# Upper table rows from GpSimd's DMA queue, four matmuls for the last half of T, more idle matmuls, a moved w_out step and two transform steps per PSUM bank

## The chip, the cores and the metric

The kernel runs on one core of a Trainium2 chip. The metric is the device time of one execution in microseconds (us), as a median over runs. PE is TensorE, DVE is VectorE, ACT is ScalarE, POOL is GpSimd, SP is the engine that issues most DMAs.

## What is computed

The reference chains three operators over 24576 rows of 256 numbers (8 sequences of 3072):

```python
X = np.fft.fft(np.fft.fft(x, axis=1), axis=2).real      # x: 8 x 3072 x 256, float32
logits = X @ phi                                        # 32 slots, 8 experts x 4
d = exp(logits - logits.max(0)); d /= d.sum(0) + 1e-9   # softmax over all tokens
slot_out[e] = maximum((d.T @ X)[e] @ w1[e], 0) @ w2[e]
c = exp(logits - logits.max(1)); c /= c.sum(1) + 1e-9   # softmax over slots
y = c @ slot_out
out = (s * maximum(y @ w_in, 0)**2 + b) @ w_out         # w_in 256 x 2048, w_out 2048 x 256, float64
```

## The kernel before, in words

The transform is not computed for 256 columns. `x` is projected with the DFT-transformed `phi` to 32 slot columns, the sequence transform is done on these, and the logits come out of it. The stages follow one another on PE:

- **V** (about 12 to 84 us). `emit_v` (L382) multiplies pages of `x` (`xb`, 1 MB each, 24 of them, three to a batch) with the projected `phi`; part 0 of a batch needs pages x0 and x2, part 1 page x1. `turn_v` (L408) transposes the result. `pump_a` (L316) issues loads in the order of the string `ORDER` (L297): x is a page of `x`, w a quarter of `w_out` (float64, turned into float32 on DVE by `double_steps`), r a page of `x` for a later stage (`xrt`), l a part of the table `ltab`, h a part of `htab`. All of these are issued on SP's queue, at most eight outstanding.
- **T.** `emit_t` (L423) does the 128-point transform of a batch and writes `tt`. For the last batch it is split: four matmuls (L428) and eight copies on ACT (L432) for the first half of the steps, 32 matmuls of a 32x32 tile each (L439) and two DVE copies (L445) for the last half. `keep_warm` (L187) issues matmuls on a tile of ones that nobody reads; `WARM` = 4 of them follow T (L519).
- **L** (90 to 106 us). 16 half steps (L570) multiply `ltab` with `tt`, the two halves of the rows (0 to 63 and 64 to 127) beside each other. Both need the same table, so the rows 64 to 127 of `ltab` are a copy of rows 0 to 63, made by POOL (L512, L513). For each half step ACT copies the PSUM bank to `lg` (L583) and DVE takes the maximum (L585).
- **The maximum** (L592 to L610). The maximum over all tokens is put together: a transpose to `mt` (L598), a reduction to `cm2` (L603), a diagonal `dg` (L605), a matmul `mb` (L607) that spreads it over the partitions, a copy to `cmb` (L608). 8, 3 and 8 idle matmuls lie between (L596, L599, L610). Ahead of `cm2`, the loop at L600 empties `side_work`: at that point it holds the two steps `low` of the last quarter of `w_out` (L216 on DVE), which also give back a page.
- **H** (114.5 to 142 us). 16 steps: `emit_d` subtracts the maximum (L633, DVE and POOL in turn), ACT takes the exponential (L669), four matmuls with a part of `htab` (L652) fill two PSUM tiles of 208 columns, and `h_out` (L639) copies one on ACT and one on DVE to `hh` (L643).
- **R** (142 to 204 us). Transposes, a transform and sums with the 24 pages `xrt` (L704 to L731); each page that is used up is loaded anew, and after the `xrt` come `w_in`, `w1` and `w2`. **E** (to 236 us) are the experts. **F** is the last operator, 64 blocks of 384 tokens, until the end at 1411.6 us.

The pages of 8 KB per partition come from a ring of 15, later 20, and a load waits until the page's last user is done. Engines run their instructions in the order in which the program issued them.

Of the kernel before, what the change touches and what calls it, by code (L numbers as in the profile page):

```python
# [32 lines left out]
def tile_fft2__then__softmoe__then__act_relu2(  # L33
# [261 lines left out]
    WARM = 4  # L295
# [50 lines left out]
    def htab_load(i):  # L346

        t, k = page([R, 16, 2, 4 * MH], F32, "htab_t")
        htabs.append((t, k))
        nc.gpsimd.memset(t[32:64], 0.0)  # L350
        for q in range(2):
            nc.sync.dma_start(out=t[64 * q:64 * q + M], in_=htab[:, 32 * i:32 * i + 32].rearrange("r (k q) m -> r k q m", q=2))
        dma_ready(2.5)
# [5 lines left out]
    def ltab_load(i):  # L359
        t, k = page([P, 32, P // 2], F32, "ltab")  # L360
        ltabs.append((t, k))
        for c in range(2):
            nc.sync.dma_start(out=t[NR * c:NR * c + NR], in_=ltab[64 * c:64 * c + M, 32 * i:32 * i + 32].rearrange(
                "(j g) q m -> g j q m", j=2)[0:NR // 2])
        dma_ready(2.57)

    with tc.tile_pool(name="xtp", bufs=1, side="right") as xtp, tc.tile_pool(name="vp", bufs=1, side="right") as vp, \
# [55 lines left out]
        def emit_t(b):  # L423
            bg, bq = divmod(b, NG)
            if b == B - 1:
# [8 lines left out]
                t = psv.tile([P, 2, 4, 64], F32, tag="vt", name="tpb", bufs=2)  # L434
                for k in range(4, 8):
                    for j in range(4):
                        for c in range(2):
                            q = 64 * (j // 2) + NR * c
                            nc.tensor.matmul(t[q:q + NR, j % 2, k - 4, :], lhsT=vs[bg][:, bq, 4 * k + j, :],  # L439
                                             rhs=f_sb[:, 64 * c:64 * c + 64], start=True, stop=True,  # L440
                                             tile_position=(0, q), skip_group_check=True)
                for eh in range(2):
                    src = t[64 * eh:64 * eh + 64].rearrange("p j k m -> p m j k")
                    dst = tt[64 * bg:64 * bg + 64, :, bq, 16 * eh:16 * eh + 16].rearrange("p m (j k) -> p m j k", j=2)
                    nc.vector.tensor_copy(dst[:, :, :, 4:8], src)  # L445
# [66 lines left out]
        nc.gpsimd.tensor_copy(ltabs[0][0][64:P], ltabs[0][0][0:64])  # L512
        nc.gpsimd.tensor_copy(ltabs[1][0][64:P], ltabs[1][0][0:64])  # L513
# [44 lines left out]
    with tc.tile_pool(name="ps_l", bufs=6, space=PSUM) as psl, \  # L558
# [37 lines left out]
        keep_warm(warm, 8)  # L596
        mt = psm.tile([NE, R], F32, tag="mt", name="mt")
        nc.tensor.transpose(mt, cm1, ident[:R, :R])  # L598
        keep_warm(warm, 3)  # L599
        while side_step(0.0, True):  # L600
            pass
# [8 lines left out]
        keep_warm(warm, 8)  # L610
# [13 lines left out]
    with tc.tile_pool(name="ps_h", bufs=3, space=PSUM) as psh:  # L624
# [14 lines left out]
        def h_out(i):  # L639
            for q in range(2):  # L640
                hpv = hps[i][q].rearrange("p k (q c m) -> p (k q) c m", q=2, c=2)
                eng = nc.vector.tensor_copy if q else nc.scalar.copy
# [667 lines left out]
```

## Time and profile before

| | us |
|---|---|
| median of three runs (1397.17 to 1401.28) | 1400.21 |
| span of the profiled execution | 1411.6 |
| of it V, T and their start (to the first L570) | 90.3 |
| L and the maximum (to the first L652) | 24.3 |
| H | 27.6 |
| R and E (to 236 us) | 94 |
| F | 1175 |

The profiled execution is one execution, and its span, from its first instruction to its last, is 11.4 us longer than the median of the runs. PE is busy in 98% of the span, but busy says nothing of the clock: the row PEclk of the page is the share of TensorE's full clock that was granted (1.00 is 2.4 GHz, 0.50 is 1.2 GHz). Its mean is 0.984, and after the first few microseconds it is below 1.00 in three stretches, all of them ahead of 145 us (and in the last microsecond).

### The profile page before, as it was taken

To read this page: it belongs to the slowest core of one execution; us is meant where nothing else is said; L and a number is where in the kernel's file an instruction comes from. 1 tells how busy PE (TensorE), PEld (TensorE's weight loads), DVE (VectorE), ACT (ScalarE), POOL (GpSimd) and SP (SyncE) were. 2 spreads that over 40 slices of the span, in tenths; PEclk is the share of its full clock that TensorE was granted. 3 is DMA by queue.
4 is the path that set the end of the run, shared out by engine and by line. 5 is a ranking of instruction groups with operands and counts; after the bars stand their busy time and mean duration, and the time that the engine had idled before them with its cause. 6 is when DMAs were issued, how large, how long until landed. Compare 5 with 4: busy or idle time off the path is not lost.

```text
span 1411.6 us, 23102 instructions
## 1 busy us (share of the span) xinstructions
PE 1388.2 (98%) x9036; PEld 856.0 (61%) x9036; DVE 1171.9 (83%) x1490; ACT 1010.7 (72%) x1423; POOL 233.1 (17%) x287
## 2 busy tenths in 40 slices
PE   8989999999999999999999999999999999999998
PEld 5669564566666666666666666666666666666665
DVE  1565764998989999999989898989898989888886
ACT  2774314877777777777877787877777777777775
POOL 1143400021212121211112121111111111111110
PEclk9995999999999999999999999999999999999999
DMA  8995795101010101101010101010101010101001
GB/s 352 414 311 229 291 414 225 29 27 36 20 36 23 36 24 29 30 23 32 23 36 21 34 23 36 23 33 23 36 23 36 23 36 23 33 23 36 23 20 30
DMA packets 72381, 112.27 MB, mean 80 GB/s; under 512 B 33904, under 2 KB 59632, under 8 KB 64976
## 3 DMA queue, kind: packets, MB, share of 16 engines
q1 hardware_dynamic: 72144, 110.70, 23.1%
q8 instruction: 71, 1.16, 0.3%
q14 instruction: 38, 0.31, 0.1%
q0 software_dynamic: 128, 0.10, 0.0%
HBM read 78.48 MB, written 25.17 MB: 73 GB/s over the span
## 4 chain that ended last, share of the span: by engine, by line
PE 88%; DMA 2%; DVE 1%; issue 1%; SPq 0%; ACT 0%; POOL 0%; DVEq 0%; ACTq 0%; POOLq 0%
PE op L1151 46%; PE op L1154 23%; PE fhp L1121 12%; PE racc L727 3%; DMA w2t<-in_moe_w_dram 2%; PE hp L652 2%; PE dps L712 1%; PE lp L570 1%; SPq L1084 0%; DVE cm L585 0%; DVE r L1127 0%; DVE rhl L1112 0%; PE eop L957 0%; DMA g<-gs 0%; PE gp L1055 0%
## 5 line engine op out<-in xcount | busy, mean ns | idle before, releaser
L1151 PE MATMUL op<-whl,rhl 128*128 128x512 f16 x3072 | 1025.3, 379 | 0.8 <-ACT rhl L1111 0.6
L1154 PE MATMUL op<-whl,rhl 128*128 128x256 f16 x3072 | 835.7, 273 | 0.0
L1126 ACT ACTIVATE r<-fhp,wsc 128x768 f32<-128x768 f32 (+1 forms) x513 | 461.8, 900 | 230.0 <-PE fhp L1121 228.8
L1127 DVE SCALAR_TENSOR_TENSOR r<-fhp,r 128x768 f32<-128x768 f32 (+1 forms) x513 | 488.9, 953 | 113.6 <-ACT r L1126 104.0
L1112 DVE TENSOR_TENSOR rhl<-r,rhl 128x768 f16<-128x768 f32 x511 | 506.9, 992 | 0.9 <-ACT rhl L1111 0.9
L1151 PEld LDWEIGHTS <-rhl 128*128 128x128 f16 x3072 | 300.5, 98 | 335.4 <-ACT rhl L1111 0.9
L1111 ACT CAST rhl<-r 128x768 f16<-128x768 f32 x511 | 420.1, 822 | 1.8 <-DVE r L1127 1.8
L1154 PEld LDWEIGHTS <-rhl 128*128 128x128 f16 x3072 | 300.6, 98 | 62.7 <-issue 0.3
L1166 POOL TENSOR_TENSOR ot<-ot,bias 128x256 f32<-128x256 f32 x189 | 138.1, 731 | 974.2 <-DVE ot L1164 974.2
L1121 PE MATMUL fhp<-ct,g 128*128 128x384 f16 x1024 | 250.4, 326 | 1.1 <-DMA g<-gs 0.8
L1121 PEld LDWEIGHTS <-g 128*128 128x128 f16 x1024 | 99.9, 98 | 69.0 <-issue 1.1
L1163 ACT ACTIVATE o<-op,small 128x256 f32<-128x256 f32 x189 | 90.0, 477 | 16.7 <-PE op L1154 16.7
L1164 DVE SCALAR_TENSOR_TENSOR ot<-op,small,o 128x256 f32<-128x256 f32 x192 | 91.7, 478 | 0.3
L394 PE MATMUL vt<-xb,phd 128*64 128x384 f32 (+3 forms) x288 | 49.0, 477 | 5.3 <-DMA xb<-in_x_turned_dram 5.3
L727 PE MATMUL racc<-xrt,dh 128*64 128x256 f32 x384 | 44.5, 383 | 0.4 <-DVE dh L717 0.4
L394 PEld LDWEIGHTS vt<-xb,phd 128*64 128x64 f32 x288 | 26.5, 139 | 25.5 <-issue 13.8
L727 PEld LDWEIGHTS racc<-xrt,dh 128*64 128x64 f32 x384 | 26.3, 137 | 20.9 <-issue 4.5
L419 DVE COPY v<-vq 128x512 f32<-128x512 f32 (+1 forms) x15 | 8.3, 593 | 33.9 <-PE vq L415 33.9
L406 ACT COPY vts<-vt 128x512 f32<-128x512 f32 (+1 forms) x16 | 8.5, 533 | 32.1 <-PE vt L394 32.0
L464 ACT COPY tt<-tps 32x512 f32<-32x512 f32 x48 | 27.7, 577 | 4.9 <-PE tps L450 4.4
L652 PE MATMUL hp<-htab_t,dt 112*128 112x104 f32 x128 | 27.6, 422 | 0.2 <-ACT dt L669 0.2
L652 PEld LDWEIGHTS hp<-htab_t,dt 112*128 112x128 f32 x128 | 27.4, 333 | 0.5 <-issue 0.5
(229 smaller groups left out, 518.0 us busy)
## 6 DMA issues: line engine op xcount, KB each, us to landing
xb<-in_x_turned_dram SPq DMA_DIRECT2D x24, 1024.0 KB, 20.1
xrt<-in_x_pages_dram SPq DMA_DIRECT2D x24, 1024.0 KB, 13.9
out_dram<-ot SPq DMA_DIRECT2D x128, 128.0 KB, 1.7
w1t<-in_moe_w_dram SPq DMA_DIRECT2D x8, 1024.0 KB, 13.7
out_dram<-ot SPq DMA_DIRECT2D x128, 64.0 KB, 2.0
raw<-in_moe_w_out_dram SPq DMA_DIRECT2D x4, 1024.0 KB, 20.3
raw<-in_moe_w_in_dram SPq DMA_DIRECT2D x4, 1024.0 KB, 7.8
w2t<-in_moe_w_dram SPq DMA_DIRECT2D x4, 1024.0 KB, 17.8
```

The lines of the kernel that those rows point to most:

```text
L652: nc.tensor.matmul(hp[q][:, k, :], start=True, stop=True, lhsT=dt.rearrange("p k g e -> p (k g e)")[:, 128 * (2 * k + q):128 * (2 * k + q) ...
L727: nc.tensor.matmul(raccs[acc][64 * h:64 * h + 64, :], lhsT=dh[:, m, g].rearrange("p j e -> p (j e)"), rhs=xr[k][0][:, g, t, :], start=(sum ...
L1111: nc.scalar.copy(a, r2)
L1112: nc.vector.tensor_tensor(out=l, in0=r2, in1=a, op=ALU.subtract)
L1121: nc.tensor.matmul(hp[k * split][:, k, :].rearrange("p (s b m) -> p s b m", s=2, b=B), lhsT=g16[:, f * P:(f + 1) * P], rhs=c, start=True, ...
L1126: nc.scalar.activation(out=r[:, k], in_=hp[i][:, k], func=AF.Relu, scale=wsc[:, 2, p:p + 1])
L1127: nc.vector.scalar_tensor_tensor(out=r2[:, k], in0=hp[i][:, k], scalar=0.0, in1=r[:, k], op0=ALU.max, op1=ALU.mult)
L1151: nc.tensor.matmul(op.rearrange("p h d -> p (h d)"), lhsT=a, rhs=w.rearrange("p h d -> p (h d)"), start=(f == 0), stop=False)
L1154: nc.tensor.matmul(op[:, 0, :], lhsT=l, rhs=w[:, 0, :], start=False, stop=(f == NFC - 1))
L1163: nc.scalar.activation(out=o1, in_=op[:, 1, :], func=AF.Copy, scale=qv)
L1164: nc.vector.scalar_tensor_tensor(out=ot, in0=op[:, 0, :], scalar=qv, in1=o1, op0=ALU.mult, op1=ALU.add)
L1166: nc.gpsimd.tensor_tensor(out=ot, in0=ot, in1=bias, op=ALU.add)
```

## The change

There are five edits.

1. The upper rows of both parts of `ltab` are no longer copied by POOL; four more DMAs of 256 KB, issued by POOL, load them from DRAM. The second of the two DMAs of each `htab` part (312 KB) also moves from SP's queue to POOL's.
2. The last half of T for the last batch takes four matmuls of 128 columns in place of 32 small ones, and eight DVE copies of 32x256 in place of two of 64x512.
3. Idle matmuls: 10 for 4 after T, 14 for 8 after L, 4 for 3 behind `mt`, 7 for 8 behind `mb`.
4. The two steps `low` that stood ahead of `cm2` are taken one by one in H, from its step 3 on.
5. In H two steps share a PSUM tile of 416 columns, and one copy empties both; in every second pair of the first PSUM tile the copy is DVE's, not ACT's. The last two steps are copied one by one.

```diff
--- before.py
+++ after.py
@@ -292,7 +292,7 @@
 
     NX = 3 * B
     CR = 1.5
-    WARM = 4
+    WARM = 10
     LEAD, TOL, LT, LX, HX = 14.0, 0.5, 0, 0, 1
     ORDER = "xxxwxxxxxxwxxxxxxwxxxxwxrllhhrr"
     tpool = tc.alloc_tile_pool(name="tpool", bufs=1)
@@ -349,7 +349,7 @@
         htabs.append((t, k))
         nc.gpsimd.memset(t[32:64], 0.0)
         for q in range(2):
-            nc.sync.dma_start(out=t[64 * q:64 * q + M], in_=htab[:, 32 * i:32 * i + 32].rearrange("r (k q) m -> r k q m", q=2))
+            (nc.gpsimd if q else nc.sync).dma_start(out=t[64 * q:64 * q + M], in_=htab[:, 32 * i:32 * i + 32].rearrange("r (k q) m -> r k q m", q=2))
         dma_ready(2.5)
 
     def htab_clear(i):
@@ -360,8 +360,10 @@
         t, k = page([P, 32, P // 2], F32, "ltab")
         ltabs.append((t, k))
         for c in range(2):
-            nc.sync.dma_start(out=t[NR * c:NR * c + NR], in_=ltab[64 * c:64 * c + M, 32 * i:32 * i + 32].rearrange(
-                "(j g) q m -> g j q m", j=2)[0:NR // 2])
+            for h in range(2):
+                r = 64 * h + NR * c
+                (nc.gpsimd if h else nc.sync).dma_start(
+                    out=t[r:r + NR], in_=ltab[64 * c:64 * c + M, 32 * i:32 * i + 32].rearrange("(j g) q m -> g j q m", j=2)[0:NR // 2])
         dma_ready(2.57)
 
     with tc.tile_pool(name="xtp", bufs=1, side="right") as xtp, tc.tile_pool(name="vp", bufs=1, side="right") as vp, \
@@ -431,18 +433,14 @@
                     for c in range(2):
                         nc.scalar.copy(tt[64 * bg + NR * c:64 * bg + NR * c + NR, :, bq, 8 * j:8 * j + 4],
                                        t[NR * j:NR * j + NR, :, 64 * c:64 * c + 64].rearrange("p e k -> p k e"))
-                t = psv.tile([P, 2, 4, 64], F32, tag="vt", name="tpb", bufs=2)
+                t = psv.tile([P, 4, P], F32, tag="vt", name="tpb", bufs=2)
                 for k in range(4, 8):
-                    for j in range(4):
-                        for c in range(2):
-                            q = 64 * (j // 2) + NR * c
-                            nc.tensor.matmul(t[q:q + NR, j % 2, k - 4, :], lhsT=vs[bg][:, bq, 4 * k + j, :],
-                                             rhs=f_sb[:, 64 * c:64 * c + 64], start=True, stop=True,
-                                             tile_position=(0, q), skip_group_check=True)
-                for eh in range(2):
-                    src = t[64 * eh:64 * eh + 64].rearrange("p j k m -> p m j k")
-                    dst = tt[64 * bg:64 * bg + 64, :, bq, 16 * eh:16 * eh + 16].rearrange("p m (j k) -> p m j k", j=2)
-                    nc.vector.tensor_copy(dst[:, :, :, 4:8], src)
+                    nc.tensor.matmul(t[:, k - 4, :], lhsT=vs[bg][:, bq, 4 * k:4 * k + 4, :].rearrange("p j n -> p (j n)"),
+                                     rhs=f_sb, start=True, stop=True)
+                for j in range(4):
+                    for c in range(2):
+                        nc.vector.tensor_copy(tt[64 * bg + NR * c:64 * bg + NR * c + NR, :, bq, 8 * j + 4:8 * j + 8],
+                                              t[NR * j:NR * j + NR, :, 64 * c:64 * c + 64].rearrange("p e k -> p k e"))
                 at["pe"] += 3.0
                 return
             t = psv.tile([P, 8, P], F32, tag="tps", name="tps", bufs=2)
@@ -509,8 +507,6 @@
             f()
         for n in range(2 * B - 2, 2 * B):
             turn_v(n)
-        nc.gpsimd.tensor_copy(ltabs[0][0][64:P], ltabs[0][0][0:64])
-        nc.gpsimd.tensor_copy(ltabs[1][0][64:P], ltabs[1][0][0:64])
         for _ in range(4):
             side_step(0.0, True)
         emit_t(B - 1)
@@ -593,12 +589,10 @@
                                             op=ALU.max)
                 done_l += 1
         warm = psl.tile([R, 2, B * NE], F32, name="lp")[:, 0, :R]
-        keep_warm(warm, 8)
+        keep_warm(warm, 14)
         mt = psm.tile([NE, R], F32, tag="mt", name="mt")
         nc.tensor.transpose(mt, cm1, ident[:R, :R])
-        keep_warm(warm, 3)
-        while side_step(0.0, True):
-            pass
+        keep_warm(warm, 4)
         cm2 = temps.tile([NE, 1], F32, name="cm2", bufs=1)
         nc.vector.tensor_reduce(out=cm2, in_=mt, axis=AX.X, op=ALU.max)
         dg = temps.tile([NE, NE], F32, name="dg", bufs=1)
@@ -607,7 +601,7 @@
         nc.tensor.matmul(mb, lhsT=ones[:NE, :], rhs=dg, start=True, stop=True)
         nc.vector.tensor_copy(cmb, mb)
         mxp[0] = None
-        keep_warm(warm, 8)
+        keep_warm(warm, 7)
         fill_stack()
 
     temps.release()
@@ -636,30 +630,33 @@
                     in1=cmb[:R].unsqueeze(1).to_broadcast([R, 16, NE]),
                 )
 
-        def h_out(i):
+        def h_out(i, n):
+            o = 4 * (i % 2)
             for q in range(2):
-                hpv = hps[i][q].rearrange("p k (q c m) -> p (k q) c m", q=2, c=2)
-                eng = nc.vector.tensor_copy if q else nc.scalar.copy
-                eng(hh[q].rearrange("p m (c k) -> p k c m", c=2)[:, KC * i:KC * i + KC], hpv)
-            hps.pop(i)
+                hpv = hps[i // 2][q].rearrange("p k (q c m) -> p (k q) c m", q=2, c=2)[:, o:o + 4 * n]
+                eng = nc.vector.tensor_copy if q or (n > 1 and i % 4) else nc.scalar.copy
+                eng(hh[q].rearrange("p m (c k) -> p k c m", c=2)[:, KC * i:KC * (i + n)], hpv)
 
         hps = {}
         for i in range(-3, NCH + 1):
             if 0 <= i < NCH:
                 dt = dts.pop(i)
-                hp = [psh.tile([P, 2, 8 * MH], F32, name=f"hp{q}") for q in range(2)]
+                if i % 2 == 0:
+                    hps[i // 2] = [psh.tile([P, 4, 8 * MH], F32, name=f"hp{q}") for q in range(2)]
+                hp = hps[i // 2]
                 for k, q in [(0, 0), (1, 0), (0, 1), (1, 1)] if i == NCH - 1 else [(0, 0), (0, 1), (1, 0), (1, 1)]:
                     nc.tensor.matmul(
-                        hp[q][:, k, :], start=True, stop=True,
+                        hp[q][:, 2 * (i % 2) + k, :], start=True, stop=True,
                         lhsT=dt.rearrange("p k g e -> p (k g e)")[:, 128 * (2 * k + q):128 * (2 * k + q) + 128],
                         rhs=htabs[i // 8][0][:, 2 * (i % 8) + k].rearrange("p q m -> p (q m)"),
                     )
                 if i % 8 == 7:
                     drop(htabs[i // 8][1])
                 pump()
-                hps[i] = hp
-            if i >= 1:
-                h_out(i - 1)
+            if i > NCH - 2:
+                h_out(i - 1, 1)
+            elif i > 0 and i % 2 == 0:
+                h_out(i - 2, 2)
             if i + 3 < NCH:
                 emit_d(i + 3)
             busy("dve", 0.6)
@@ -667,6 +664,10 @@
             if 0 <= i + 2 < NCH:
                 for h in ks(i + 2):
                     nc.scalar.activation(out=dts[i + 2][:, h], in_=dts[i + 2][:, h], func=AF.Exp)
+            if i > 2:
+                side_step(0.0, True)
+        while side_step(0.0, True):
+            pass
     temps.release()
 
 
```

## Rows read from the trace of the kernel before

**Rows 1.** Windows by stage: us, each engine's busy time (instructions), granted clock, DMA share, GB/s

```profile
60.00:80.00 20.00, 19.57 (x133) 12.87 (x129) 12.18 (x17) 14.84 (x27) 5.87 (x6) 1.00 1.02 410
```

**Rows 2.** Windows of half a microsecond, the same columns: where the clock falls

```profile
96.50:97.00 0.50, 0.00 (x0) 0.00 (x0) 0.20 (x1) 0.00 (x0) 0.50 (x1) 0.58 0.75 259
...
110.00:110.50 0.50, 0.06 (x1) 0.06 (x1) 0.28 (x2) 0.00 (x0) 0.00 (x0) 0.73 1.01 426
```

**Rows 3.** Chain that ended last, in order of time: start, us, what

```profile
95.01 3.88 issue
...
105.58 0.73 DVE cm L589
...
108.14 0.42 DVE cm L592
108.56 1.32 DVE whl L216 x2
...
110.44 0.65 PE mb L607 x2
...
114.55 27.61 PE hp L652 x128
...
203.89 18.57 DMA w2t<-in_moe_w_dram
```

**Rows 4.** Timeline, the end of V, T and L: start, us, engine, line

```profile
60.43 1.73 SPq L289 DMA_DIRECT2D xb<-in_x_turned_dram  x1
...
81.28 2.38 PE L394 MATMUL vt<-xb,phd 128*64 128x384 f32 x20
...
86.52 1.12 PE L439 MATMUL tpb<-f_sb,v 128*32 128x64 f32 x64
...
87.22 2.98 ACT L432 COPY tt<-tpa 32x256 f32<-32x256 f32 x8
...
87.57 1.16 PE L190 MATMUL warm<-ones 128*128 128x128 f32 x8
...
88.19 1.39 DVE L445 COPY tt<-tpb 64x512 f32<-64x512 f32 x2
...
90.25 3.94 PE L570 MATMUL lp<-tt,ltab 64*64 64x128 f32 x114 [1.52 <-ACT tt L432]
...
92.20 4.50 DVE L585 TENSOR_REDUCE cm<-lp 112x32 f32<-112x512 f32 x7 [2.61 <-ACT lg L583]
```

**Rows 5.** The tile xb: time from the issue of its 24 loads to landing

```profile
DMA to landing us min/median/max: 10.3/20.1/20.5
```

**Rows 6.** Timeline of POOL in V

```profile
54.90 3.15 POOL L276 TENSOR_TENSOR bias<-bias,wo 128x256 f32<-128x256 f32 x4 [15.45 <-DVE wo L174]
63.59 1.48 POOL L350 MEMSET htab_t<- 32x1664 f32 x1 [5.54 <-PE vt L394]
```

**Rows 7.** DMA issues around 200 us: KB each, us from issue to landing

```profile
sel_sb<-in_sel_dram POOLq DMA_DIRECT2D x1, 32.0 KB, 6.7
```

**Rows 8.** Window while the table rows land, columns as in rows 1

```profile
92.00:94.00 2.00, 2.00 (x80) 1.95 (x69) 1.68 (x3) 1.77 (x5) 1.90 (x1) 1.00 1.03 195
```

**Rows 9.** DMA queues from 96 to 98 us: packets, MB, share of 16 engines

```profile
q8 instruction: 1, 0.02, 3.7%
```

**Rows 10.** Groups by line and form in H: busy us, mean ns, idle before

```profile
L652 PE MATMUL hp<-htab_t,dt 112*128 112x104 f32 x128 | 27.6, 422 | 0.2 <-ACT dt L669 0.2
...
L669 ACT ACTIVATE dt<-dt 112x512 f32<-112x512 f32 x14 | 8.8, 627 | 0.0
L643 ACT COPY hh<-hp 128x208 f32<-128x208 f32 x16 | 8.2, 514 | 13.5 <-PE hp L652 13.5
L633 DVE TENSOR_TENSOR dt<-lg,cmb 112x512 f32<-112x512 f32 x6 | 4.1, 676 | 0.0
```

**Rows 11.** Windows from H's middle to R's end, columns as in rows 1

```profile
122.00:146.00 24.00, 23.60 (x109) 22.48 (x108) 10.39 (x21) 11.80 (x25) 8.24 (x7) 0.53 0.26 96
...
158.00:203.00 45.00, 45.00 (x368) 25.69 (x366) 34.31 (x44) 5.38 (x10) 2.91 (x3) 1.00 0.99 394
```

## The prediction

> **What bounds the kernel now.** I read the clock first, then the chain, then what feeds it. F, from 236 us on, is PE at full clock without gaps; the change doesn't touch it. So the question is by how much the first 236 us move. They have four limits in turn. Up to 81 us it is the DMA: its share is full and it moves 410 GB/s [rows 1]. The last page of `x` was issued at 60.43 and such loads take up to 20.5 us to land, so it landed at about 80.9; PE takes it up at 81.28 [rows 4, 5]. PE has 0.4 us of slack there. L is limited by DVE, whose maxima follow each other at 4.50 / 7 = 0.643 us [rows 4], until PE stops at 95.01 for 3.88 us with "issue", a wait for nothing that the profile shows [rows 3]. An instruction packet of 16 KB goes over the DMA engines at the end of just that stop [rows 9]: I read it as PE waiting for its next instructions. In the stop the clock falls to half [rows 2], and it falls again at 110.2, when PE had idled for most of the maximum's chain. From there H runs on PE alone at 1.2 GHz: 27.61 us [rows 3], PE busy in all of it, ACT's copies waiting 13.5 us for PE [rows 10]. Being busy there didn't bring the clock back. In the rest, R frees pages and the DMA fills them; its share is 0.26 from 122 to 146, because no page is free, and 0.99 from 158 to 203 [rows 11]. The chain then waits for `w2` to land [rows 3]. What R starts earlier, `w2` lands earlier, as long as DMA idle time is left: 24 x 0.74 = 17.8 us in that one window.
>
> **Tables from POOL.** Added are six DMA issues on POOL. POOL passes the place of the `ltab` issues at 54.90 + 3.15 = 58.05 and that of the first `htab` part at 63.59 + 1.48 = 65.07 [rows 6], while SP, eight loads deep, comes to its own twenty microseconds later. Queued behind them on POOL are memsets and bias sums nobody waits for at that time. A POOL load does not stand behind SP's: one of 32 KB landed in 6.7 us [rows 7], against the 20 us of rows 5. So 4 x 256 + 2 x 312 = 1648 KB (1.69 MB) pass through the engines ahead of the last page of `x`, of which 1 MB is new traffic. At 410 GB/s that is 4.1 us; at the 195 GB/s at which transfers to a part of the partitions run [rows 8] it is 8.7. Below nothing it can't be, the DMA being full. I take 5.4, nearer the first, since wide loads run beside them, less the slack of 0.4: V ends **5.0 later**. PE waits for pages around 68 us, and if that costs the clock for a while it is up to 1.7 more; I take **+1.0**. Removed are two POOL copies, which no wait on PE shows: 0. The `htab` halves that leave SP's queue shorten it behind the last page, which is hidden by the pages R has in hand.
>
> The Trainium skill speaks against this edit: "Trainium Kernel Development and Optimization", Key Constraints, has DMAs from SP, ACT and POOL run on the same 16 engines and interleave, so that a further queue saves only issue time. By that rule the term stays at 4.1 or more; were POOL's loads queued behind SP's, it would be 0 and the sum 5 us better. Row 7's 6.7 us sides with the rule.
>
> **T.** PE's time is even: eight full passes cost 1.16 us (the idle ones after T are such), the 64 small ones 1.12 [rows 4]. But DVE makes eight copies for two. ACT's copies of this shape take 2.98 / 8 = 0.37 us [rows 4]; eight are 3.0 against 1.39. DVE begins at 88.19 [rows 4], so it would end at 91.2, where ACT ends at 90.2 and L begins at 90.25: **+1.0**. The ten idle matmuls end before that and hold nobody up. A pass is two instructions, a weight load and a matmul: PE has 128 - 16 = 112 fewer here and, with two passes for an idle matmul, 24 more for `WARM`, so block boundaries move 88 instructions further into L's 512.
>
> **L.** If the next block is there in time, 16 maxima from 92.20 take 10.3, and with 0.73 and 0.42 [rows 3] L ends at 103.65, not 108.56: **-4.9**. In favour: the boundary comes later, PE runs up to six banks ahead of DVE, so that a stop of two microseconds hides, and the table section is shorter on SP's queue. Against: the same block size, the same full DMA. The ends are 0 and -4.9; I take -4.9.
>
> **The maximum.** `low` holds DVE from 108.56 to 109.88 [rows 3], and `cm2` needs only a transpose meanwhile, for which I give 0.45 of the 1.32 (estimate): `cm2` is 0.85 earlier. At full clock `mb` (0.65) and the idle matmuls up to 114.3 shrink; H now begins 3.46 after `mb` (111.09 to 114.55 [rows 3]); then it waits for a subtraction of 0.68, an exponential of 0.63 [rows 10], the copy `cmb` and hand-overs, 1.75 (estimate). With the halved `mb` that is 2.0 more. Together **-2.85**.
>
> **H.** At full clock four matmuls take half of 27.61 / 16 = 1.73, so 0.86 a step. ACT: 0.63 exponential a step, and a pair copy every fourth step. A copy of 416 columns isn't in the trace; its ends are 0.51, a copy of half its size, and twice that [rows 10]; I take 0.88, nearer the second, since `hh` is written with a stride. ACT then needs 0.63 + 0.22 = 0.85. DVE (I give its copies ACT's duration): three pair copies and two subtractions of 0.68 in four steps, 1.0 a step, and the two `low`, 1.3, which come here. So DVE is the limit: 16 x 1.0 + 1.3 and some latency, 18.0, range 16.5 to 19.5: **-9.6**. R's first matmuls, now at 0.5, give another 1 (estimate, the window's mean is 0.53 [rows 11]): **-1.0**.
>
> **Sum.** 5.0 + 1.0 + 1.0 - 4.9 - 2.85 - 9.6 - 1.0 = -11.35. On the profiled execution this is 1411.6 to 1400.3; on the median 1400.21 to **1388.9**. Shift at R's start is passed on to `w2` in full, 11.35 being under 17.8.
>
> **The rivals.**
>
> *The clock isn't held (slower).* One mechanism: PE's block of instructions is late in L again. POOL's extra megabyte doesn't shorten the full DMA stretch, and the new boundary, 88 instructions further, is again inside L. If PE stands for as long as before (3.88 us, [rows 3]), the clock falls in L, and H starts at half. Then L and H stay, and of the gains only `low`'s 0.85 is left: 5 + 1 + 1 - 0.85 = +6.2, **1406.4**; with POOL's loads at 195 GB/s +9.5. It decides at the stop which outlasts DVE's backlog of about 2 us. For it: the page loads are as dense. Chance 0.19.
>
> *L is mended but the chain of the maximum isn't.* PE idles at `mb` (the next boundary falls near it by my count), the clock drops there, H is 27.6: 7 - 4.9 - 0.85 = +1.2, **1401.5**, same. In the kernel before PE had 3 idle matmuls, 0.9 us, behind `mt` and the clock fell all the same. Against: 14 of them, at 1.16 / 4 = 0.29, now stand ahead of `mt`, 4.1 us for the 3.0 that DVE needs (105.58 to 108.56 [rows 3]). Chance 0.17.
>
> *The timed runs never had the slow H.* The profiled execution is 11.4 us longer than the median, about what H at half clock costs; the place at which the clock is lowered may differ between executions. Then H was at ACT's 16 x 1.14 = 18.3 already, and only L, `low` and 0.3 in H remain: 7 - 4.9 - 0.85 - 0.3 = +1, **1401.2**, same. Against: the runs lie within 0.3% of each other, and PE stands still for 3.88 us in L whenever the block is late. Chance 0.22.
>
> On that gap the Trainium skill has a figure ("Runtime: NRT & Kernel Launch", on the preamble and postamble): a profile's total is longer than the executed time by about 6.2 us for any kernel. By it only 5 us of the 11.4 are open, too little for H at half clock, and this rival would lose half its chance; no run here shows it, so I leave the 0.22.
>
> **How the numbers follow.** The forecast has 0.42, with its own range of 1384.5 to 1394 from H's bounds (1.5 either way), POOL's (4.1 to 8.7) and the clock in V (0 to 1.7). The rivals have 0.19, 0.17 and 0.22. The range runs from 1384.5 through all but the slowest of these, 1405.5; outside it lies about half of the first rival and a tail below. A measurement of this kernel can tell about 0.3% (4.2 us) from no change. Faster is the forecast and some of the third rival's spread, 0.45; same, the middle two, 0.36; slower 0.19.
>
> **What would show it.** In the profile after: PEclk at 1.00 from L to R's start; no "issue" stop over 2 us in L570; H near 18 us with DVE nearly full and PE waiting; the last L394 of V beginning at about 86, not 81.3, with the wait laid on `xb`; DVE copies of T ending after ACT's. If L394 isn't late, POOL's loads don't overtake SP's and I am 5 us too high. If H is 27 us at 0.50, the first two rivals are told apart by whether the stop is in L or behind it. I am wrong on the size if pair copies cost over 1.0, as DVE then sets H at 19 or more.

## The result

The changed kernel takes 1418.79 us (median of 4 runs, 1413.9 to 1421.72) against 1400.74 us before (4 runs, 1397.17 to 1402.53): a ratio of 1.0134, 95% interval 1.0115 to 1.0152. It is **slower by 1.3%**, 18 us. The forecast was 1388.9, its range ended at 1405.5, and the slowest rival stood at 1406.4, or 1409.7 with POOL's loads at 195 GB/s.

The profiled execution of after has a span of 1415.5 us, and its own time is 1417.4. One thing about before has to be known to read what follows: the profiled execution shown ahead of the prediction was an exception. Its span of 1411.6 us stands for a time of about 1413.5 (an estimate: in the other runs the time is 1.7 to 2.0 us above the span), 13 us above the median. A second profile of the same kernel (the run base_again) has a span of 1396.7 us and the time of the other runs. Of the 112 executions of the kernel before that ran beside the experiments, 107 took 1395 to 1406 us, three took 1413 to 1416 us at a mean granted clock of 0.984 to 0.985 (the exception had 0.984), and two took over 3700 us. The comparisons below are therefore with base_again.

The profile after, by views, with the group of before that each answers to. Window from 60 to 80 us (columns as in [rows 1]):

```profile
60.00:80.00 20.00, 10.01 (x63) 6.61 (x61) 7.06 (x9) 8.32 (x15) 3.45 (x5) 0.74 1.03 296
```

PE was busy for 19.57 of these 20 us and is now busy for 10; the DMA's share is as full as before, but it moves 296 GB/s in place of 410. The timeline of PE in V, and the DMA issues from 55 to 90 us (KB each, median us to landing), answer to [rows 4, 5, 7]:

```profile
77.70 7.68 PE L396 MATMUL vt<-xb,phd 128*64 128x384 f32 x32 [9.99 <-DMA xb<-in_x_turned_dram]
...
93.62 2.38 PE L396 MATMUL vt<-xb,phd 128*64 128x384 f32 x20
```

```profile
xb<-in_x_turned_dram SPq DMA_DIRECT2D x3, 1024.0 KB, 29.7
...
ltab<-in_ltab_dram POOLq DMA_DIRECT2D x4, 256.0 KB, 9.1
```

PE stands 10 us for a page of `x`; pages that took 20.1 us to land take 29.7, while POOL's rows land in 9.1. V's last group, at 81.28 in [rows 4] and at 81.79 in base_again, begins at 93.62. The same rows of base_again, with L's start, its two stops and `mt`:

```profile
68.47 4.95 PE L394 MATMUL vt<-xb,phd 128*64 128x384 f32 x32 [0.51 <-DMA xb<-in_x_turned_dram]
...
81.79 2.37 PE L394 MATMUL vt<-xb,phd 128*64 128x384 f32 x20
...
90.74 1.37 PE L570 MATMUL lp<-tt,ltab 64*64 64x128 f32 x18 [1.50 <-ACT tt L432]
...
98.90 2.64 PE L570 MATMUL lp<-tt,ltab 64*48 64x128 f32 x86 [1.92 <-issue]
...
105.19 0.43 PE L570 MATMUL lp<-tt,ltab 64*64 64x128 f32 x4 [1.74 <-issue]
...
108.68 0.38 PE L598 MATMUL mt<-ident,cm 112*32 112x112 f32 x1
```

T and L after (timeline; [rows 3, 4]):

```profile
99.55 2.98 ACT L434 COPY tt<-tpa 32x256 f32<-32x256 f32 x8
...
100.78 3.47 DVE L442 COPY tt<-tpb 32x256 f32<-32x256 f32 x8
...
104.46 6.02 PE L566 MATMUL lp<-tt,ltab 64*64 64x128 f32 x167 [2.41 <-ACT whl L212]
...
111.46 3.10 PE L566 MATMUL lp<-tt,ltab 64*48 64x128 f32 x89 [0.98 <-issue]
...
118.10 0.27 PE L594 MATMUL mt<-ident,cm 112*32 112x112 f32 x1 [0.60 <-DVE cm L588]
```

DVE's eight copies end at 104.25, and L begins at 104.46. (The row lays PE's wait on ACT's `whl`, which by the view ended at 103.89; DVE's copies are what came last.) The stop of 3.88 us in L ([rows 3]; two stops of 1.92 and 1.74 in base_again) is down to 0.98. H (timeline, then its two parts as windows, then its groups; [rows 3, 10]):

```profile
121.27 7.89 PE L648 MATMUL hp<-htab_t,dt 112*128 112x104 f32 x64 [0.21 <-DMA xrt<-in_x_pages_dram]
...
125.37 1.93 POOL L627 TENSOR_TENSOR dt<-lg,cmb 112x512 f32<-112x512 f32 x1 [0.42 <-PE hp L648]
125.43 0.74 DVE L216 SCALAR_TENSOR_TENSOR whl<-wo,wsc,whl 128x512 f16<-128x512 f32 x1
...
127.34 0.63 ACT L666 ACTIVATE dt<-dt 112x512 f32<-112x512 f32 x1 [1.16 <-POOL dt L627]
127.55 1.66 DVE L216 SCALAR_TENSOR_TENSOR whl<-wo,wsc,whl 128x512 f16<-128x512 f32 x1
...
130.52 13.56 PE L648 MATMUL hp<-htab_t,dt 112*128 112x104 f32 x64 [1.37 <-ACT dt L666]
```

```profile
121.00:130.50 9.50, 7.94 (x65) 7.45 (x64) 9.16 (x11) 6.34 (x12) 8.04 (x6) 1.00 0.87 359
130.50:144.50 14.00, 13.88 (x66) 13.62 (x67) 7.42 (x12) 6.57 (x11) 3.00 (x3) 0.52 0.42 158
```

```profile
L638 DVE COPY hh<-hp 128x416 f32<-128x416 f32 x10 | 8.3, 874 | 3.1 <-PE hp L648 3.1
L627 DVE TENSOR_TENSOR dt<-lg,cmb 112x512 f32<-112x512 f32 x7 | 7.2, 1035 | 1.2 <-PE hp L648 1.2
...
L216 DVE SCALAR_TENSOR_TENSOR whl<-wo,wsc,whl 128x512 f16<-128x512 f32 x2 | 2.4, 1198 | 0.0
```

H's first 64 matmuls (records of the trace, two to each matmul of the program) take 7.89 us at full clock. DVE is full (9.16 of 9.5 us) with the two `low` steps of line 216 in its queue, an exponential comes late, PE stands 1.37 us for it, the granted clock falls to half, and the other 64 matmuls take 13.56 us. H is 22.81 us long.

Now H in base_again (its window, its groups):

```profile
112.00:127.00 15.00, 14.72 (x129) 14.59 (x130) 11.64 (x23) 14.13 (x31) 9.64 (x8) 1.00 0.94 390
```

```profile
L652 PE MATMUL hp<-htab_t,dt 112*128 112x104 f32 x128 | 14.6, 276 | 0.2 <-DMA xrt<-in_x_pages_dram 0.2
...
L643 DVE COPY hh<-hp 128x208 f32<-128x208 f32 x16 | 8.3, 520 | 3.4 <-PE hp L652 3.2
L643 ACT COPY hh<-hp 128x208 f32<-128x208 f32 x16 | 8.0, 514 | 0.0
```

In the kernel before as it normally runs, H is 14.57 us at full clock, limited by PE itself. There were 13 us less to gain than the profile of [rows 3] showed.

Stage by stage, from the start of one stage to the start of the next in the timelines of base_again and after, beside the forecast (V's last group counts from its first matmul; the expectations below count from its second, 0.3 to 0.4 us later):

| stage | forecast | base_again | after | difference |
|---|---|---|---|---|
| V, to its last group | +6.0 | 81.79 | 93.62 | +11.8 |
| T, from there to L | +1.0 | 8.95 | 10.84 | +1.9 |
| L, to `mt` | -4.9 | 17.94 | 13.64 | -4.3 |
| maximum, `mt` to H | -2.85 | 3.44 | 3.17 | -0.3 |
| H | -9.6 | 14.57 | 22.81 | +8.2 |
| H's end to R's first sum | -1.0 | 3.53 | 4.87 | +1.3 |
| sum | -11.35 | | | +18.7 |

From R on nothing differs: R's first sum comes 18.7 us later, the end of the span 18.8.

### The profile page after: what moved, and what is told of

It is laid out like the page before. It is cut to its first block, busy times and chain, and to the rows that moved or that the text cites. A ratio compares the mean times of both kernels' runs of the same rounds, so it can differ in the third digit from the quotient of the medians.

```text
span 1415.5 us, 23041 instructions
## 1 busy us (share of the span) xinstructions
PE 1384.3 (98%) x9004; PEld 850.3 (60%) x9004; DVE 1177.1 (83%) x1492; ACT 1008.2 (71%) x1413; POOL 233.6 (17%) x291
## 4 chain that ended last, share of the span: by engine, by line
PE 88%; DMA 9%; DVE 2%; SPq 1%; ACT 0%; issue 0%; DVEq 0%; ACTq 0%
PE op L1152 46%; PE op L1155 23%; PE fhp L1122 12%; DMA xb<-in_x_turned_dram 4%; PE racc L728 3%; DMA w2t<-in_moe_w_dram 2%; DMA htab_t<-in_htab_dram 1%; DMA xrt<-in_x_pages_dram 1%; PE hp L648 1%; PE dps L713 1%; PE vt L396 1%; SPq L1085 1%; PE tps L448 0%; DVE r L1128 0%; DVE rhl L1113 0%
## 5 line engine op out<-in xcount | busy, mean ns | idle before, releaser
L396 PE MATMUL vt<-xb,phd 128*64 128x512 f32 (+3 forms) x288 | 50.6, 488 | 13.6 <-DMA xb<-in_x_turned_dram 13.5
L775 POOL TENSOR_TENSOR lg<-lg,rm 112x512 f32<-112x512 f32 x16 | 22.5, 1408 | 8.8 <-DVE rm L773 8.8
L648 PE MATMUL hp<-htab_t,dt 112*128 112x104 f32 x128 | 21.4, 347 | 1.6 <-ACT dt L666 1.4
## 6 DMA issues: line engine op xcount, KB each, us to landing
xb<-in_x_turned_dram SPq DMA_DIRECT2D x24, 1024.0 KB, 20.1
xrt<-in_x_pages_dram SPq DMA_DIRECT2D x24, 1024.0 KB, 13.7
```

Source lines behind the costliest of these rows:

```text
L396: nc.tensor.matmul(vt[64 * h:64 * h + 64, o:o + k, :], lhsT=phd[:, c, sg, :], rhs=turned(pg, c, i, k, rev), start=(c == 0 and m < 2), stop ...
```

## The experiments

Times are medians, ratios those to the kernel before on the same chip, with 95% intervals. The edits have the numbers of the section on the change.

### The kernel before once more, and the change in two halves

**base_again** is the kernel before, unchanged.

> The kernel before, unchanged, for the state of its clock. The changed kernel's runs lie 1.9 us above their spans, so the profiled execution of the kernel before (span 1411.6) stands for about 1413.5 us, while its timed runs gave 1397 to 1403. Theory A (the timed runs of before keep the clock through H, the profiled one lost it): spans of 1395 to 1401 at a mean clock of 0.99 or more, H at 17 to 20 us in its trace if the profiled execution is of that kind. Theory B (profiling itself lengthens the execution): a trace with H at 27 to 28 us and a clock of 0.984 in executions that are timed at 1400.

1398.91 us, 0.9985 (0.997 to 1.0). H 14.57 us at full clock, as shown above, below the 17 to 20 expected: the third rival was right that before's timed runs don't have the slow H. It had H at 18.3, because it added ACT's copies and exponentials up. They overlap, as ACT's timeline of base_again shows: the copy starts 0.54 us after an exponential of 0.63, the next exponential 0.31 us after a copy of 0.51, and the pair takes 0.85 us, not 1.14.

```profile
117.37 0.63 ACT L669 ACTIVATE dt<-dt 112x512 f32<-112x512 f32 x1
117.91 0.51 ACT L643 COPY hh<-hp 128x208 f32<-128x208 f32 x1
118.22 0.63 ACT L669 ACTIVATE dt<-dt 112x512 f32<-112x512 f32 x1
```

**pool_only** is the kernel before with edit 1 alone (in the edits below `[...]` stands for the rest of an expression):

```diff
-            nc.sync.dma_start(out=t[64 * q:64 * q + M], in_=htab[...])
+            (nc.gpsimd if q else nc.sync).dma_start(out=t[64 * q:64 * q + M], in_=htab[...])
...
-            nc.sync.dma_start(out=t[NR * c:NR * c + NR], in_=ltab[...])
+            for h in range(2):
+                r = 64 * h + NR * c
+                (nc.gpsimd if h else nc.sync).dma_start(out=t[r:r + NR], in_=ltab[...])
...
-        nc.gpsimd.tensor_copy(ltabs[0][0][64:P], ltabs[0][0][0:64])
-        nc.gpsimd.tensor_copy(ltabs[1][0][64:P], ltabs[1][0][0:64])
```

> The kernel before with edit 1 alone (upper table rows and half of htab from GpSimd's queue). Theory A (GpSimd's loads pass ahead of the last pages of x and slow all transfers while they run): the last L394 of V begins near 93 us instead of 81, time 1408 to 1416. Rival (the other four edits cost the time): 1399 to 1403.

1410.35 us, 1.0065 (1.0046 to 1.0084). V's last group starts at 95.53, 13.7 us late; H is 14.51 us. The time is as theory A said, V's delay above its estimate; L, 1.9 us shorter than in base_again, gives some of it back. So edit 1 alone costs 10.7 us of the 18 and has no part in H.

**no_pool** is the change with that edit undone.

> The change without edit 1 (tables as in the kernel before, the two GpSimd copies back). Theory A: V ends as in before (last product of V at 81 us), L without a stop of over 2 us, time 1394 to 1403, so that nearly all of the 18 us lost come from edit 1. Rival (H with two steps per bank and w_out's low part in it loses the time): 1408 or more.

1407.56 us, 1.0052 (1.0034 to 1.007). That is between the two theories, and rightly so: V ends as in before (its last group at 82.25), as A had it, but H is 22.20 us with the same stop. By the medians 10.7 and 7.9 make 18.6, the whole loss; by the ratios 0.65% and 0.52% make 1.17% of the 1.34%, within their intervals. There are two causes, and they add.

**sp_upper** is the whole change with every table load on SP's queue (the line of the H table is changed in the same way):

```diff
-                (nc.gpsimd if h else nc.sync).dma_start(
+                nc.sync.dma_start(
```

> The change with all table loads on SP's queue: the same bytes as the change, the upper rows still from DRAM, but behind the pages of x. Theory A (it is the overtaking): V ends near 81 us, tables land some 2 to 4 us later than in before, time 1396 to 1406. Rival (it is the extra megabyte and the narrow transfers wherever they are issued): 1412 or more.

1409.04 us, 1.0055 (1.0038 to 1.0072). V's last group is back at 83.17, and the time is 1.5 us above no_pool's, within what the two spread. It misses A's 1406 by H's stop, which is in it (H 21.77 us), not by V. The extra megabyte costs little if it stands behind `x`, though L's stop is 3.81 us in this profile against 1.17 in no_pool's.

### What in edit 1 costs

**pool_late** is pool_only with one POOL instruction ahead of each `ltab` part, so that POOL's loads wait for the last page of `x`:

```diff
         ltabs.append((t, k))
+        nc.gpsimd.tensor_copy(small[:, 20 + i:21 + i], xa[-1][0][:, 0, 0, 0:1])
```

> Edit 1 alone on the kernel before, with one more GpSimd instruction ahead of each table's loads: it reads a word of the last page of x, so that GpSimd issues its table loads only when that page has landed. Bytes, queues and shapes are those of edit 1 alone (1410.4 us, last V group started at 95.9 against 82.1 in the kernel before). Theory A (the loads cost because they overtake the last pages of x): the last V group starts at 81.5 to 84 again; the tables are then read behind V, 1 MB more of them, so L starts 2 to 6 us later than the 90.7 of before (sp_upper: 94.0), and the time is 1401 to 1406. Rival B (GpSimd's queue or the extra megabyte costs wherever it runs): 1408 or more.

1399.23 us, 0.9984 (0.9956 to 1.0013): no loss is left, and V's last group starts at 80.46. Same bytes, same queue, same shape, 22 us later (POOL's timeline, pool_late):

```profile
79.95 0.72 POOL L362 COPY small<-xb 128x1 f32<-128x1 f32 x1 [23.04 <-DMA xb<-in_x_turned_dram]
80.62 1.23 POOL L366 DMA_DIRECT2D ltab<-in_ltab_dram  x2
```

That the loads overtake the last pages of `x` is the cause. I had expected a price behind V of 2 to 6 us; there was none: from V's last group to L it is 8.96 us, in base_again 8.95.

**pool_wide** lays the L table out in DRAM with its rows already twice, so that each part is one load to all 128 partitions, from POOL's queue at edit 1's place (the H table as in before):

```diff
-        for c in range(2):
-            nc.sync.dma_start(out=t[NR * c:NR * c + NR], in_=ltab[...])
+        nc.gpsimd.dma_start(out=t, in_=ltab[:, 32 * i:32 * i + 32])
```

> The kernel before with the L table laid out in DRAM with its rows already twice, so that each of its two parts is one load of 1024 KB to all 128 partitions; GpSimd issues both where edit 1 issues its first loads; no GpSimd copies, the H table as before on SyncE. 2048 KB pass ahead of the last pages of x in place of the 1648 KB of edit 1, all in wide loads. Theory A (edit 1's 13.8 us in V come from the narrow shape, loads to 32 and 48 partitions at which the DMA moved 195 to 240 GB/s at full share): at 410 GB/s 2 MB are 5.1 us, the last V group starts at 86 to 88.5, the window 60 to 80 us moves over 390 GB/s, and the time is 1402 to 1406. Rival B (loads from GpSimd's queue are slow or slow the others, whatever their shape): the rate falls to about 200 to 300 GB/s again, V starts its last group at 92 or later, 1408 or more.

1401.70 us, 1.0003 (0.9976 to 1.0029), a little below theory A's range. The windows from 60 to 80 us of pool_only, pool_wide and pool_late, in this order:

```profile
60.00:80.00 20.00, 8.71 (x59) 5.80 (x57) 5.99 (x8) 8.62 (x16) 2.90 (x4) 0.79 1.03 269
```

```profile
60.00:80.00 20.00, 13.23 (x81) 8.28 (x79) 8.06 (x11) 8.76 (x16) 4.52 (x6) 0.83 1.02 413
```

```profile
60.00:80.00 20.00, 19.53 (x136) 13.14 (x132) 12.45 (x17) 14.72 (x26) 0.05 (x1) 1.00 1.03 411
```

More bytes than edit 1's (2048 KB for 1648) overtake `x`, and the DMA still moves 413 GB/s; V is late by 7.5 us (its last group at 89.28), not 13.7. So it is the narrow loads (to 32 and 48 partitions) that take the DMA from 411 to 269 GB/s, for the pages beside them too, and POOL's queue as such does not. What pool_wide changes beside the width isn't taken apart: one load for each part in place of four, the order of the rows in DRAM, and an H table that stays on SP's queue. V's 7.5 is above the 5.1 of theory A and below its rival's bound. PE takes up the awaited page 6.1 us later than in base_again (74.55 against 68.47), of which 2 MB at 410 GB/s explain 5.1; and as the clock had fallen while PE waited, the 32 matmuls behind it take 6.38 us for 4.95, another 1.4.

### What in H costs

**np_single** is no_pool with edit 5 undone: one copy a step on ACT and on DVE, `low` still in H.

> The change without edit 1 and without edit 5: H's steps write a bank each again, with one copy each on ACT and DVE; the two low steps of w_out stay in H. Theory A (the copies of two steps make H's stop: 0.87 us each, three of four on DVE): H is 14.5 to 16.5 us at full clock as in the kernel before, against 22.2 with edit 5, and the time is 1398 to 1402 (1407.6 less 6 to 8). Rival B (the two low steps in DVE's queue, 0.74 and 1.66 us, make it): H keeps a stop of over 1 us and 20 us or more, 1405 or more.

1405.97 us, 1.0021 (0.9992 to 1.0051). H is 22.45 us with a stop of 1.00 us (PE's timeline of np_single):

```profile
119.59 13.45 PE L646 MATMUL hp<-htab_t,dt 112*128 112x104 f32 x64 [1.00 <-ACT dt L663]
```

Theory A, that the copies of two steps make the stop, falls. Seven of its ten runs took 1404.6 to 1408.1 us, at mean granted clocks of 0.990 to 0.994, and three 1399.0 to 1400.2, at 0.996 to 0.998: in those three the clock was not lost for long, if at all. Why not no trace shows; the profile is of one of the seven.

**np_low** is no_pool with edit 4 undone instead: `low` ahead of `cm2`, copies of two steps.

> The change without edit 1 and without edit 4: the two low steps stand ahead of cm2 again; H's copies take two steps at a time. Theory A (the copies of two steps alone fill DVE, 1.0 us a step against PE's 0.87): H still has its stop, or is limited by DVE at 16 to 17 us without one; low ahead of cm2 costs 0.9 before H; time 1403 to 1408. Rival B (low makes the stop, the copies are harmless): H 14 to 15.5 us at full clock, 1398 to 1401.

1401.58 us, 1.0008 (0.998 to 1.0037), H 14.95 us. (Its profiled execution, 1410.48 us, had a late page in V; the other nine runs lie between 1400.1 and 1404.4.) Rival B was right in H, its time a little low.

**np_tail** leaves everything of no_pool and moves only `low`, behind H's loop:

```diff
-            if i > 2:
-                side_step(0.0, True)
         while side_step(0.0, True):
             pass
```

> The change without edit 1, and the two low steps issued behind H's loop in place of inside it; H's copies still take two steps at a time. Theory A (low's place in DVE's queue among H's subtractions makes H's stop, and the stop costs the clock): H is 14.5 to 15.3 us without a stop over 0.4 us and without half clock, against 22.2; low then costs at most its own 1.5 us of DVE at R's start, and the time is 1398 to 1402 (1407.6 less 6 to 9). Rival B (the copies of two steps leave H at its limit, and np_low's 14.95 was an exception): H above 16 us, 1403 or more.

1398.61 us, 0.9989 (0.9968 to 1.001), 9.0 us below no_pool; H 14.94 us at full clock. Its groups in H:

```profile
L648 PE MATMUL hp<-htab_t,dt 112*128 112x104 f32 x128 | 14.9, 278 | 0.2 <-DMA xrt<-in_x_pages_dram 0.2
...
L638 DVE COPY hh<-hp 128x416 f32<-128x416 f32 x10 | 8.3, 888 | 0.0
L627 DVE TENSOR_TENSOR dt<-lg,cmb 112x512 f32<-112x512 f32 x7 | 7.6, 1082 | 0.3 <-PE hp L648 0.3
...
L638 DVE COPY hh<-hp 128x208 f32<-128x208 f32 x1 | 0.5, 506 | 0.9 <-PE hp L648 0.9
```

With the copies of two steps DVE is idle for 0.3 + 0.9 = 1.2 us in H, and the 0.9 come just before its last copy; in base_again it is idle for 3.4. The two `low` took 2.4 us in after.

**np_spread** and **single_spread** ask whether `low` can be hidden in H at all: its two steps six steps apart, with the copies of two steps and with single ones.

```diff
-            if i > 2:
+            if i in (3, 9):
                 side_step(0.0, True)
```

> The change without edit 1, the two low steps inside H but six steps apart (after step 3 and after step 9) in place of after steps 3 and 4; H's copies take two steps at a time. In np_tail, with low behind H, DVE had 1.2 us idle in H's 14.9. Theory A (DVE's queue has no room: 2.1 to 2.4 us of low do not fit into 1.2): H keeps a stop, if smaller, or runs 16 us or longer, and the time is 1401 to 1407. Rival B (only the neighbourhood of the two steps makes the stop, each alone is hidden by the steps that ACT is ahead): H 14.9 to 15.6 us, 1397.5 to 1400.5.

1402.05 us, 1.0016 (1.0006 to 1.0026). H is 17.75 us, with stops but at full clock (PE's timeline of np_spread):

```profile
111.96 7.89 PE L648 MATMUL hp<-htab_t,dt 112*128 112x104 f32 x64 [0.21 <-ACT dt L666]
120.61 3.96 PE L648 MATMUL hp<-htab_t,dt 112*128 112x104 f32 x32 [0.76 <-ACT dt L666]
125.33 2.03 PE L648 MATMUL hp<-htab_t,dt 112*128 112x104 f32 x16 [0.76 <-ACT dt L666]
127.68 2.03 PE L648 MATMUL hp<-htab_t,dt 112*128 112x104 f32 x16 [0.32 <-ACT dt L666]
```

Apart from each other, the two `low` take 0.74 us each (DVE's timeline of np_spread), the second no longer 1.66:

```profile
116.12 0.74 DVE L216 SCALAR_TENSOR_TENSOR whl<-wo,wsc,whl 128x512 f16<-128x512 f32 x1
...
124.53 0.74 DVE L216 SCALAR_TENSOR_TENSOR whl<-wo,wsc,whl 128x512 f16<-128x512 f32 x1
```

> As np_spread, but H's copies take one step each, one on ACT and one on DVE: in the kernel before DVE had 3.4 us idle in H's 14.6. Theory A (room in DVE's queue decides): low's 2.1 us fit when they are apart, H is 14.6 to 15.3 us at full clock and the time 1397.5 to 1401, while np_spread is over 1401. Rival B (low stretches GpSimd's subtraction beside it, so that any low in H makes PE stop): a stop of over 0.5 us in H and in most runs 1403 to 1408, like np_single.

1398.32 us, 0.9996 (0.9979 to 1.0012); H 15.43 us at full clock, just above theory A's 15.3, the longest time from the start of one matmul to the next 0.41. (In its profiled execution, 1403.62 us, V was late, its last group starting at 87.39; eight of the ten runs took 1395.3 to 1401.3.) Theory A holds in both: `low` fits where DVE has room and its steps stand apart. Without room it costs 2.8 us in H at full clock (17.75 less 14.94, of it stops of 1.84); with both steps in a row it costs 7.3 (no_pool's 22.20 less 14.94), most of it the half clock behind a stop of 1.36: no_pool's last 64 matmuls take 12.96 us, its first 64 7.88.

### The harmless edits, and two attempts at more

**t_idle** is the kernel before with edits 2 and 3 alone.

> The kernel before with edits 2 and 3 alone: T's last half in four matmuls and eight DVE copies, and the idle matmuls. Theory A (the two edits cancel): L starts 2 us later than the 90.7 of before, at 92.8 as without edit 1, because of DVE's eight copies; L's PE part ends 1 to 1.5 us earlier, its 2.2 us stop being gone; H begins within 0.7 us of the 112.1 of before at full clock and lasts 14.5 to 15; the time is 1398 to 1401.5. Rival B (the eight copies are a loss that nothing gives back): H begins 2 us later, 1401.5 to 1404. Rival C (idle matmuls keep a clock that the timed runs did lose in some executions): 1394 to 1397.

1399.76 us, 0.9987 (0.9962 to 1.0011). L starts at 93.00 and H at 111.74: what the eight copies lose, L gives back. Its `mt` to H takes 4.00 us, np_tail's 3.16, with `low` behind H: `low` ahead of `cm2` costs 0.84 us there.

**late_tail** joins pool_late, edits 2 and 3, and `low` behind H; **wide_tail** the same with pool_wide's table on SP's queue at its old place.

> All of the change that the runs so far show harmless, with its two costs mended: the table rows come from GpSimd's queue but only when the last page of x has landed, the low steps stand behind H's loop, H's copies take one step each, T's four matmuls and the idle ones are in. Theory A: V ends as in the kernel before (82.8), L starts at 90 to 92, H begins at 108.5 to 110.5 against 112.1 and lasts 14.6, and what H gains reaches the end: 1395.5 to 1399 against 1399.6. Rival B (low behind H delays R by its 1.5 us, and the gain is lost there): 1399 to 1401.5.

1402.08 us, 1.0013 (0.9993 to 1.0033): a miss. L begins at 95.26, and PE stops again with "issue" in it (late_tail, PE's timeline):

```profile
105.42 4.77 PE L567 MATMUL lp<-tt,ltab 64*48 64x128 f32 x89 [2.79 <-issue]
```

> As late_tail, but the L table's rows lie twice in DRAM and each of its parts is one SyncE load of 1024 KB to all 128 partitions, at the place of the narrow loads of before; the H table as before. Theory A (the narrow shape is what costs): the tables land behind the last page of x at 400 GB/s, about 5 us sooner for H's table and R's pages; L starts at 90 to 92 as T sets it, H begins at 108 to 110.5; 1395 to 1399. Rival B: the tables' landing hid already behind T and L, low behind H takes back the gain: 1399 to 1401.5.

1398.34 us, 0.9984 (0.9964 to 1.0004). L begins at 93.79 and H at 112.20, against 93.00 and 111.74 in t_idle with the narrow loads: L did not wait for the table's landing. No version measured is faster than the kernel before beyond the measurement.

L's stop is 0.98 us in after, 2.79 in late_tail and 3.81 in sp_upper, with the same instructions on PE. The traces tell how far this can be explained: they hold 17 such stops of L over 0.6 us ("issue", in 15 of the 16 traces), and each ends 1.2 to 1.6 us after a packet of the instruction queue (q8, as in [rows 9]) has landed. In after the packet starts 1.5 us ahead of the stop, at 108.94, lands at 110.04, and PE goes on at 111.46; in sp_upper it starts 1.1 us behind the stop's beginning, at 101.16, lands at 102.41, and PE goes on at 103.84. That fits the prediction's reading, PE waiting for its next instructions. Why the packet comes earlier or later is not settled, and no run isolates it.

## Why the prediction was wrong

Three steps failed: H was costed as if the timed runs had it at half clock, the narrow loads were sized too small, and the two `low` in H were costed without the stop and the lost clock that they bring. The steps in the prediction's own order; the table above has the terms.

**What bounds the kernel now** was wrong for H, and this is the largest piece: 13.0 us of the 30 between forecast and result (27.61 in the profile, 14.57 in base_again). I built the sum on one execution whose H ran at half clock, and gave "the timed runs never had the slow H" 0.22 against it, on the grounds that the runs agree within 0.3% and that PE stands in L whenever the block is late. The agreement was evidence for the rival: a kernel that loses its clock at a place that varies would not agree so well, and the profile was 11.4 us above the median. The second ground doesn't hold either: sp_upper stands for 3.81 us in L, the clock falls there (0.82 from 100 to 104 us), and its H begins at full clock. Why the profiled execution lost its clock ahead of H, and held it at half throughout, stays open. L's term needed the same care: base_again has two stops of 1.92 and 1.74 us there, not one of 3.88. The 6.2 us that the Trainium skill ("Runtime: NRT & Kernel Launch", on preamble and postamble) puts between a profile's total and the executed time don't carry over to the span of these traces: after's own time is 1.9 us longer than its span, not shorter.

**Tables from POOL**: the mechanism was right, the size was not. POOL's loads overtake SP's, as [rows 7] said; pool_late shows it by taking it away. Predicted 6.0 with the clock, measured 11.8, and 13.7 in pool_only. The failed step is the price of the 1648 KB, "nearer the first, since wide loads run beside them". It was the other way: the wide loads beside them slow down too, and 269 GB/s in pool_only, at full share, is below the mean of my two ends. The row of [rows 8], 195 GB/s, was the one to go by, and even its 8.7 us bounded the term too low: PE takes up the awaited page at 77.70 in after and at 68.47 in base_again, 9.2 us later, where the forecast had 5.0. The clock's part was too small as well: behind the wait the 32 matmuls take 7.68 us for 4.95 (granted clock 0.64), 2.7 more, where the forecast had 1.0 and at most 1.7. The Trainium skill ("DMA: Bandwidth & Descriptors", Rules for kernel authors) advises one load to 128 partitions in place of two to disjoint halves, because the halves share the engines. pool_wide's 413 GB/s against pool_only's 269 agrees with the advice; that the rate itself falls beside narrow loads is what these runs add.

**T**: the eight copies were priced at 0.37 us each, from ACT's row. DVE's take 0.43, and its queue held a step of `w_out` ahead of them; 1.9 in place of 1.0.

**L**: -4.9 forecast, -4.3 measured; the stop shrank to 0.98. In t_idle it is -3.2, in late_tail -0.2 and in sp_upper +0.5, all with the same edits in T and L: that PE's stop was as short as 0.98 us in after was partly luck.

**The maximum**: -2.85 forecast, -0.3 measured. 2.0 of the forecast were the half clock of the profiled execution. `low`'s 0.85 is there between t_idle and np_tail (0.84), but not against base_again: there `low` ends at 108.33, ahead of `mt` at 108.68, and so cost nothing.

**H**: the sum per step was near, though not as near as it looks. DVE's limit of "16 x 1.0 + 1.3" is 18.0, and np_spread has 17.75, but two errors cancel there: without `low` np_tail's H takes 14.94 with DVE busy from one end of its middle to the other (12.00 us of 112 to 124), or 0.93 a step, not 1.0, and `low` adds 2.8, not 1.3. The copy of two steps, estimated at 0.88, takes 0.87. Two things were missed. First, 18.0 is a loss against H as it normally is, 14.57. Second, `low` was costed at 1.3 us as if it were spread evenly; two steps in a row, the second of 1.66 us, hold up the subtractions of DVE behind them, then an exponential, then PE for 1.37 us, and the clock goes with it: 22.81. That a stop of PE can cost the clock was rival 1, but only for L; I named no such rival for H, where the change itself loads DVE.

**R's start**: no gain to come. base_again needs 3.53 us there at full clock (1.00), and after, whose H ends at half clock, 4.87 (granted clock 0.59 from 144.1 to 149.0 us): +1.3.

Why the second `low` took 1.66 us: the first took 0.74, and POOL's subtraction beside it 1.93; beside the second POOL's took 1.28, about its shortest (1.27 in no_pool). One of the two engines seems to wait for the other. The Trainium skill ("GPSIMD Engine Reference", 1. Specifications) has GpSimd and VectorE share an SBUF interface, with contention where a DVE instruction has two SBUF inputs; `low` and the subtractions have. The durations agree with it; no run isolates it, so it stands as a reading.

## What to carry to other kernels

Before costing a change, set the profiled execution's own time beside the median: where it is 1% longer, cost every term on the median's clock, or give that reading of the profile the larger chance. A load from a second queue did not wait behind the first queue's here: in a stretch bound by DMA put it behind the last load that somebody waits for, and expect that loads to 32 or 48 partitions slow the whole DMA, not only themselves (269 GB/s for 410). Work moved "into" a stage needs idle time on that very engine, between the two instructions where it stands: 1.2 us of room did not take 1.5 (np_spread), and 3.4 us of room took it in two pieces (single_spread) but not in one (np_single).

## What was not expected of the hardware

- H's 128 matmul records take 14.6 us at 2.4 GHz and 27.6 at 1.2, with PE busy throughout in both. In after the granted clock fell behind a stop of 1.37 us in H's middle and stayed at half to H's end, though PE was busy for 13.88 of 14.00 us. In np_single it fell behind a stop of 1.00 us. Three stops of 0.76, 0.76 and 0.32 us in np_spread did not lower it.
- Narrow loads on a second queue took the DMA from 410 to 269 GB/s at the same full share, and pages of the other queue from 20.1 to 29.7 us to land.
- ACT starts an instruction before the one ahead of it has run its listed duration: 0.63 and 0.51 us follow each other in 0.85.
